# Moving output stores, gating steps and adapter preparation in a fused attention and mixture-of-adapters kernel

## The chip, the cores and the metric

The kernel runs on one core of a Trainium2 chip. The time is device microseconds of one launch. A core has five engines that each work through an instruction list of their own, in order: TensorE (PE, its weight loads shown apart as PEld), VectorE (DVE), ScalarE (ACT), GpSimd (POOL) and SyncE (SP, which here only issues DMAs). They wait for each other through semaphores. DMAs can be issued from the queues of SP, ACT and POOL.

## The reference

Two stages. The first is attention with a relative position bias, for 8 batches, 8 heads, 576 positions and 64 values per head. The second sends each of the 4608 rows of 512 values through the two best of 8 low-rank adapters (rank 16) and adds the result to the row.

```python
scores = scale * np.matmul(q, k.transpose(0, 1, 3, 2))
scores = scores + bias.transpose(2, 0, 1)[None]     # bias_table[bucket(|i - j|)], per head
attn = softmax(scores)                              # over the last axis
x = np.matmul(attn, v).transpose(0, 2, 1, 3).reshape(B * S, H * D)
logits = x @ w_gate                                 # 8 adapters
topk = two largest logits of each row; w = softmax of these two
out = x + sum over the two: w * ((x @ A[e]) @ B[e])
```

## The kernel before, in words

**Units and slots.** The work is cut into 32 units, one for each batch and pair of heads (four units to a batch). A unit has six slots, s0 to s5. The program is written out slot by slot, by hand, in a loop over `t` (192 slots); every engine gets its instructions in that order. `scores` opens each slot: matmuls into one of two PSUM buffers `sc`, and one exponential on ACT that empties it. Slots s0, s1, s3 and s4 have the large exponential (128x1024, line 344), s2 the `pe` tile of the last 64 keys (line 363), s5 the remaining 64 queries (line 348). In unit 0 the small ones come in the other order.

**What follows the scores.** The bias is a multiplication of the exponentials by a table `eb` (line 374, DVE, both operands bfloat16 in SBUF, 512 or 768 elements per partition; `bias_tail` at 383). The table is made once: a row `gx` goes to DRAM (`gx_d`, line 731, ACT's queue) and comes back spread over the partitions (`table_load`, line 193, SP). `values` (line 409) multiplies probabilities and values in half-tiles of 64 keys; `whole` (line 431) does so with 128 keys at once and was used for the last unit alone. `normalise` (441, 442) divides by the row sums.

**Loads.** SP issues all loads of q, k and v, 128 KB for a head as a rule, in the order in which `load` lists them, two or three to a slot. Staging has two buffers a batch long. POOL casts to bfloat16 into `qkn` (line 146), `vm` (151), `qke` (156) and `ve` (159), in program order; from unit 4 on, `cast_v(u)` stands in s1, the q part of unit u + 2 in s2 and its k part in s3. PE transposes them (283) in the slots before their unit and DVE copies the result out (287).

**Adapters.** `load_adapters` fetches A (`Af`), the gate (`Gf`) and B (`Bf`), on SP, while the second batch is being loaded. `cast_adapters(0)` makes `A4` on POOL (lines 254, 256) in unit 4, s4. `order_pe` (264) puts A's rows into the order needed, with matmuls against a spread identity, and `order_out` (268, DVE) copies that to `AW`. Those four steps enter `queue` at unit 5, s0.

**The groups of the second stage.** When a batch is done its 4 or 5 row tiles form a `Group`. Its steps go into `queue`: `front` (transposes, 473 and 479), two `sums` (486, 495, then `MAX8` at 497 and the mask at 500), `turn` (transpose of the gated sums, 528 and 533) and `back` (537, then 558 on DVE into `ot`). PE takes one step in s0, s2 and s5; DVE does its part at the next of s0, s1, s3. `enqueue` puts `pauses`, or left-over steps of the group before, between them so that the gating can be done. The gating list is popped once a slot: `distances` on POOL (509 to 511) in the slot after the mask, `gates` two slots later, which holds the tanh on ACT (517) and three POOL operations (518 to 521).

**Stores.** `dl_out` puts a store into `stores`, and the end of the next slot issues it (line 553): on POOL's queue, in the last unit on SP's. `ot` has six buffers. After the last slot, `dl_own` and `Last` finish the last rows.

Of the kernel before, what the change touches and what calls it, by code (L numbers as in the profile page):

```python
# [14 lines left out]
ALU = mybir.AluOpType  # L15
# [18 lines left out]
def kernel(  # L34
# [56 lines left out]
    def load(b):  # L91

        q32 = stg.tile([128, 4, H, D], FP32, name="q32", tag="q32")
        k32 = stg.tile([128, 4, H, D], FP32, name="k32", tag="k32")
        v32 = stg.tile([128, 4, H, D], FP32, name="v32", tag="v32")
        qke32 = stg.tile([128, H, D], FP32, name="qke32", tag="qke32")
        ve32 = stg.tile([128, HP, D], FP32, name="ve32", tag="ve32")
        staged[b] = (q32, k32, v32, qke32, ve32)
        sync = nc.sync.dma_start

        def tiles(t, src, h, j0=0, j1=4):
            return lambda: sync(out=t[:, j0:j1, h, :], in_=src[  # L102
                b, h, j0 * 128:j1 * 128, :].rearrange("(j p) d -> p j d", p=128))
# [12 lines left out]
        tail_qk = [lambda i=i, src=src: sync(out=qke32[i * 64:(i + 1) * 64],  # L116
                                             in_=src[b, :, 512:, :].rearrange("h p d -> p h d"))
                   for i, src in enumerate((q, k))]
        tail_v = [lambda i=i: sync(out=ve32[i * 64:(i + 1) * 64], in_=v[
            b, :, 512:, :].rearrange("(g two) p d -> two p g d", two=2)[i]) for i in range(2)]  # L120
        table = lambda hp: [lambda: table_load(hp)]
        values_left[b] = (values_of(2), values_of(3))
        if b:
            v2, v3 = values_left[b - 1]
            todo = v2 + (table(3) if b == 1 else []) + qk(0) + tail_qk + v3 + qk(1)
            if b == 1:
                todo += [lambda: load_adapters(0), lambda: load_adapters(1)]
            todo += values_of(0) + tail_v + qk(2) + values_of(1)
            if b == 1:
                todo += [lambda: load_adapters(2)]  # L130
            return todo + qk(3)
        return [lambda: nc.scalar.dma_start(
                    out=k32[:, 0, :2, :], in_=k[b, :2, :128, :].rearrange("h p d -> p h d")),
                tiles(q32, q, 0), tiles(q32, q, 1),
                lambda: nc.scalar.dma_start(out=btT, in_=bias_table.rearrange("b h -> h b")),
                tiles(k32, k, 0, 1), tiles(k32, k, 1, 1),
                *tail_qk, *qk(1), *values_of(0), *tail_v, *qk(2), None,
                *table(0), *table(1), *values_of(1), near_load, *qk(3), *table(2)]

    nats, tails = {}, {}  # L140

# [272 lines left out]
    def whole(u, j):  # L414

        b, hp = units[u]
        pm, pe = probs[u]
        vm, ve = vals[b % 2]
        if j == 4:
            accs[u] = pvp.tile([128, 2, 512], FP32, name="pv", tag="pv")  # L420
        pv = accs[u]
        for t in range(5):
            tok = min(t * 128, S - 128)
            for h in range(2):
                if j < 4:
                    lhsT = pm[:, h, j * S + tok:j * S + tok + 128]
                    rhs = vm[:, j, 2 * hp + h, :W]
                else:
                    keys = slice(h * 64, (h + 1) * 64)
                    lhsT, rhs = pe[keys, tok:tok + 128], ve[keys, hp, :W]  # L430
                nc.tensor.matmul(pv[:, h, t * W:(t + 1) * W], lhsT=lhsT, rhs=rhs,
                                 start=(j == 4 and t == 0), stop=(j == 3),
                                 skip_group_check=True)

    def normalise(u):
# [18 lines left out]


    queue, stores = deque(), []
    state = {"now": [], "last": None, "gating": []}

    class Group:
        def __init__(self, tiles):  # L460
# [30 lines left out]
        def zl_out(self, t0, n):  # L491
# [6 lines left out]
            if t0 + n == self.n:  # L498
                self.mk = self.tile("mk", E)
                nc.vector.tensor_tensor(self.mk, self.z[:, :, ER:], self.largest(1), op=ALU.is_ge)  # L500
                state["gating"] = [None, self.distances, None, self.gates]

        def largest(self, i):
            return self.top[:, :, i].to_broadcast((128, self.n, E))
# [1 line left out]
        def distances(self):  # L506
# [3 lines left out]
            eng.tensor_tensor(d2, lg, self.largest(1), op=ALU.subtract)  # L510
            eng.tensor_tensor(self.df, d1, d2, op=ALU.add)

        def gates(self):

            n, eng = self.n, nc.gpsimd
            th, d, gate = (self.tile(x, E) for x in ("th", "dm", "gate"))
            nc.scalar.activation(th, self.df, ACT.Tanh, scale=0.5)
            eng.tensor_tensor(d, th, self.mk, op=ALU.mult)
            eng.tensor_tensor(gate, d, self.mk, op=ALU.add)
            self.zt = self.tile("zt", ER, BF16).rearrange("p n (e r) -> p n e r", e=E)  # L520
            eng.tensor_tensor(
# [57 lines left out]
    def enqueue(tiles):  # L579
# [4 lines left out]
        steps = gr.front()  # L584
        sums1, sums2, turn = gr.middle()
        pauses = lambda n: [old.pop(0) if old else (None, None) for _ in range(n)]
        wait = 3 - len(steps) if tiles[0][0] else 3
        steps += pauses(wait) + [sums1, sums2] + pauses(7 - len(steps) - wait) + [turn]
        queue.extend(steps + old + gr.back())

    def step_pe():
        if queue:
# [127 lines left out]
            ready.append(units[p][0])  # L720

    loading = deque(todo + load(1))
    for t in range(SLOTS * NU):
        u, s = divmod(t, SLOTS)
        b, hp = units[u]
        p = u - 1
        early = u < HP
        done, stores[:] = stores[:], []
        scores(u, s)
        if t == 0:  # L730
            nc.scalar.dma_start(out=g, in_=gxe)
        if u == 0:
# [14 lines left out]
        if s == 0:  # L747
            if u == 1:
                cast_tail_v(0, pool_cast)
            if u == 5:  # L750
                queue.extend((lambda i=i: order_pe(i), lambda i=i: order_out(i))
                             for i in range(4))
            if u == 7:
                cast_adapters(1)
            if u in (1, 2):
                for j in range(2 * u - 2, 4):
                    bias(p, j)
                bias_tail(p)
            elif u:
                bias(p, 2)  # L760
# [27 lines left out]
        if s == 4:  # L788
            if u > 2:
                values(p, 1, 0, 1, 2, 3)  # L790
            if u == 4:
                cast_adapters(0)
            if early:
                transpose_pe(u + 1)
            elif u + 1 < NU:
                transpose_out(u + 1)
        if s == 5:
            if u in (1, 2):
                values(p, 1, 0, 1, 2, 3)
            if early:  # L800
                transpose_out(u + 1)
# [76 lines left out]
```

## Time and profile before

| | |
|---|---|
| median of 3 runs | 221.46 us (220.71 to 222.06) |
| the profiled execution | 221.52 us, of which the span 219.7 us |
| first exponential starts, last one ends | 7.5 us, about 201.2 us |
| busy: PE, DVE, ACT, POOL | 183.0, 172.6, 172.2, 107.1 us |
| large exponential (L344), each | 1.02 us, next one about 0.9 us after its start |
| POOL's stores (L553) | 27 issues, 559 ns each |
| granted TensorE clock, mean | 0.973 |
| DMA | 40.36 MB, 184 GB/s over the span |

A page row has the engine, what the group writes and reads, its count, its busy time and its idle time with what ended that. Three more views are used. The timeline lists instructions with their start and length and, in brackets, the idle time before them with its releaser. The view of waits sums who waited for whom. The windows view gives busy time, clock and DMA share of chosen stretches. A "unit" in the text starts at its first exponential on ACT.

### The profile page before, as it was taken

Reading aid. Unit: us, or ns where it says so; the run is one execution under the profiler, and the core shown is the slowest. Engines: PE = TensorE matmul, PEld = TensorE weight load, DVE = VectorE, ACT = ScalarE, POOL = GpSimd, SP = SyncE. Lnnn points to the kernel's source line nnn. Section 1 sums busy time; section 2 is a strip of 40 time slices with the busy share of each in tenths; the row PEclk is TensorE's granted clock in tenths of the full one; section 3 lists DMA queues with packets and bytes.
Section 4 is the critical chain, followed back from the end, with each engine's and each line's share of the span. In section 5 each row is a group of like instructions: output and inputs, shape, how many; then the busy total and the mean of one; then the engine's idle time right before and its main releaser. Section 6 shows DMA issues by size and latency. Waiting matters only on the chain.

```text
span 219.7 us, 10377 instructions
## 1 busy us (share of the span) xinstructions
PE 183.0 (83%) x4532; PEld 126.5 (58%) x4532; DVE 172.6 (79%) x356; ACT 172.2 (78%) x218; POOL 107.1 (49%) x203
## 2 busy tenths in 40 slices
PE   0869887299879999889995998989999998887851
PEld 0326565177657776557664765656777765666630
DVE  4327857138778989999989899999999999995460
ACT  4875889069779899879995899879998998888422
POOL 1562233634555729553968069535965495332010
PEclk9999999669999999999999999999999999999978
DMA  6999887989789979899898989998899421113406
GB/s 123 212 212 200 197 176 158 236 171 195 178 189 201 232 179 240 198 266 222 224 243 239 198 185 237 193 252 215 200 231 247 103 101 48 67 48 98 179 35 219
DMA packets 121189, 40.36 MB, mean 184 GB/s; under 512 B 116208, under 2 KB 118000, under 8 KB 121144
## 3 DMA queue, kind: packets, MB, share of 16 engines
q1 hardware_dynamic: 118560, 33.06, 67.6%
q0 software_dynamic: 2032, 6.56, 8.5%
q8 instruction: 35, 0.57, 1.1%
q10 hardware_dynamic: 552, 0.08, 0.2%
q14 instruction: 10, 0.08, 0.1%
HBM read 29.97 MB, written 9.45 MB: 179 GB/s over the span
## 4 chain that ended last, share of the span: by engine, by line
PE 44%; DVE 30%; SPq 15%; issue 4%; POOL 2%; ACT 2%; DMA 1%; DVEq 0%; ACTq 0%; POOLq 0%
DVE pm L374 14%; PE pv L409 11%; PE sc L334 10%; SPq L102 10%; DVE xn L442 4%; PE tp L283 4%; DVE ot L558 4%; PE xT_ps L473 3%; PE zl L486 3%; PE sc L356 3%; PE sc L317 2%; PE dl L537 2%; DVE qkT L287 2%; SPq L116 2%; DVE xT L479 1%
## 5 line engine op out<-in xcount | busy, mean ns | idle before, releaser
L344 ACT ACTIVATE pm<-sc 128x1024 bf16<-128x1024 f32 x128 | 127.4, 1023 | 29.3 <-PE sc L334 16.9
L374 DVE TENSOR_TENSOR pm<-pm,eb 128x768 bf16<-128x768 bf16 (+1 forms) x98 | 71.6, 754 | 6.7 <-DMA eb<-gx_d 3.3
L334 PE MATMUL sc<-qkT 64*128 64x64 bf16 (+1 forms) x512 | 62.6, 297 | 3.8 <-ACT pm L344 1.0
L409 PE MATMUL pv<-vm,pm 64*128 64x65 bf16 x2480 | 49.5, 191 | 1.4 <-DVE pm L374 1.3
L409 PEld LDWEIGHTS <-pm 64*128 64x128 bf16 x2480 | 44.6, 95 | 2.6 <-DVE pm L374 2.0
L334 PEld LDWEIGHTS <-qkT 64*128 64x128 bf16 x512 | 21.5, 94 | 25.6 <-issue 12.9
L146 POOL CAST qkn<-q 128x512 bf16<-128x512 f32 x31 | 21.2, 683 | 14.1 <-PE pv L409 4.7
L442 DVE TENSOR_TENSOR xn<-pv,rc 128x640 bf16<-128x640 f32 x32 | 26.4, 824 | 1.1
L553 POOL DMA_DIRECT2D out_dram<-ot x27 | 15.1, 559 | 24.6 <-DVE ot L558 24.6
L287 DVE COPY qkT<-tp 128x1024 bf16<-128x1024 bf16 x31 | 21.1, 680 | 6.6 <-PE tp L283 6.6
L317 PE MATMUL sc<-tb,turn 64*64 64x127 bf16 (+1 forms) x360 | 26.1, 218 | 0.0
L151 POOL CAST vm<-v 128x512 bf16<-128x512 f32 x32 | 21.4, 667 | 7.4 <-DMA v<-in_v_dram 7.4
L146 POOL CAST qkn<-k 128x512 bf16<-128x512 f32 (+1 forms) x32 | 20.0, 625 | 9.7 <-DMA k<-in_k_dram 9.7
L363 ACT ACTIVATE pe<-sc 128x576 bf16<-128x576 f32 x32 | 20.9, 654 | 2.5 <-PE sc L317 1.5
L283 PE MATMUL tp<-ident,qkn 128*128 128x128 bf16 x248 | 20.1, 226 | 0.0
L348 ACT ACTIVATE pm<-sc 128x512 bf16<-128x512 f32 x32 | 19.0, 593 | 0.3 <-PE sc L334 0.3
L283 PEld LDWEIGHTS <-qkn 128*128 128x128 bf16 x248 | 14.6, 100 | 7.5 <-issue 7.3
L317 PEld LDWEIGHTS <-turn 64*64 64x64 bf16 (+1 forms) x360 | 16.6, 99 | 3.6
L356 PE MATMUL sc<-qkT 64*64 64x64 bf16 (+1 forms) x128 | 16.3, 308 | 1.3 <-ACT pm L344 1.3
L509 POOL TENSOR_TENSOR da<-z,top 128x32 f32<-128x32 f32 (+1 forms) x7 | 1.8, 256 | 30.3 <-DVE top L497 30.3
L558 DVE TENSOR_TENSOR ot<-dl,xn 128x512 f32<-128x512 f32 x24 | 15.8, 681 | 0.0
L537 PE MATMUL dl<-Bc,zT 128*128 128x512 bf16 x31 | 12.0, 387 | 2.3 <-DVE zT L533 1.3
(110 smaller groups left out, 194.9 us busy)
## 6 DMA issues: line engine op xcount, KB each, us to landing
q<-in_q_dram SPq DMA_DIRECT2D x64, 128.0 KB, 4.1
k<-in_k_dram SPq DMA_DIRECT2D x62, 128.0 KB, 4.0
out_dram<-ot POOLq DMA_DIRECT2D x23, 256.0 KB, 4.1
v<-in_v_dram SPq DMA_DIRECT2D x32, 128.0 KB, 3.8
v<-in_v_dram SPq DMA_DIRECT2D x16, 256.0 KB, 5.4
out_dram<-ot SPq DMA_DIRECT2D x5, 256.0 KB, 2.2
qke<-in_q_dram SPq DMA_DIRECT2D x8, 128.0 KB, 5.0
qke<-in_k_dram SPq DMA_DIRECT2D x8, 128.0 KB, 4.4
```

The costliest lines, as they stand in the source:

```text
L102: return lambda: sync(out=t[:, j0:j1, h, :], in_=src[b, h, j0 * 128:j1 * 128, :].rearrange("(j p) d -> p j d", p=128))
L146: eng(out=nats[u][:, i, j0:j1].rearrange("p j (h d) -> p j h d", h=2), in_=staged[b][i][:, j0:j1, 2 * hp:2 * hp + 2, :])
L283: nc.tensor.transpose(ps[:, i, j, :], nats[u][:, i, j, :], ident)
L287: nc.vector.tensor_copy(batch_tiles(b)[:, hp, :, :512], tps.pop(u).rearrange("p i j t -> p i (j t)"))
L317: nc.tensor.matmul(out(a, e), lhsT=turn[rows, cols], rhs=tb[rows, hp, a - k0 + 127:e - k0 + 127], start=False, stop=True, skip_group_check ...
L334: nc.tensor.matmul(sc[:, h, o:o + n], lhsT=kT[rows, j * 128:(j + 1) * 128], rhs=qT[rows, q0:q0 + n], start=True, stop=True, skip_group_che ...
L344: nc.scalar.activation(pm[:, :, s * S:s * S + SW], sc, ACT.Exp, scale=scale)
L356: nc.tensor.matmul(flat[rows, q0:q0 + n], lhsT=kT[rows, 512:], rhs=qT[rows, q0:q0 + n], start=True, stop=True, skip_group_check=True)
L374: nc.vector.tensor_tensor(t, t, e, op=ALU.mult)
L409: nc.tensor.matmul(pv[:, h, t * W:(t + 1) * W], lhsT=lhsT, rhs=rhs, start=(j == js[0] and t == 0 and not cross), stop=(j == 3 and cross == 1),
L442: nc.vector.tensor_tensor(_ap(xs[b], hp * 128, [[D, 2], [Dm, 5], [1, D]]), _ap(pv, 0, [[512, 2], [W, 5], [1, D]]), _ap(rc, 0, [[5, 2], [1, ...
L558: nc.vector.tensor_tensor(ot, self.dl.pop(t), self.x[t], op=ALU.add)
```

## The change

1. Stores are issued from ACT's queue, two slots after they are made and behind that slot's exponential; the last unit's stores too. Only the stores behind the last slot stay on SP. POOL issues none.
2. Gating: `distances` stands one slot later, and the tanh is a step of its own, two slots behind it (one slot later than before; in the last unit as before). The POOL part of `gates` follows one slot behind the tanh.
3. Adapters: the loads of A and gate stand behind unit 6's q and k (before: ahead of that batch's first v), and B's behind unit 7's. `cast_adapters(0)` moves from unit 4, s4 to unit 5, s4, so behind the casts `vm`(5), q(7) and k(7) on POOL; B's cast moves from unit 7 to 8. The four order steps are no longer queued at unit 5: they stand in the first group's own list, between its transposes and its sums. This puts the first at unit 6, s0, and the group's first `sums` and its `turn` later too.
4. Unit 0's values: one run of `whole` in unit 1, s5 (50 matmuls) in place of `values` in s2 and s5 (100). The tile j = 0 comes first.
5. At the start, the first table load stands ahead of the two k loads of unit 2 (before: behind them).

```diff
@@ load @@
             todo = v2 + (table(3) if b == 1 else []) + qk(0) + tail_qk + v3 + qk(1)
+            todo += values_of(0) + tail_v + qk(2)
             if b == 1:
                 todo += [lambda: load_adapters(0), lambda: load_adapters(1)]
-            todo += values_of(0) + tail_v + qk(2) + values_of(1)
+            todo += values_of(1) + qk(3)
             if b == 1:
                 todo += [lambda: load_adapters(2)]
-            return todo + qk(3)
+            return todo
...
-                *tail_qk, *qk(1), *values_of(0), *tail_v, *qk(2), None,
-                *table(0), *table(1), *values_of(1), near_load, *qk(3), *table(2)]
+                *tail_qk, *qk(1), *values_of(0), *tail_v, *qk(2)[:2], None,
+                *table(0), *qk(2)[2:], *table(1), *values_of(1), near_load, *qk(3), *table(2)]
@@ Group @@
-                state["gating"] = [None, self.distances, None, self.gates]
+                state["gating"] = [None] * state["apart"] + [self.distances, None, self.tanh, self.gates]
...
+        def tanh(self):
+            self.th = self.tile("th", E)
+            nc.scalar.activation(self.th, self.df, ACT.Tanh, scale=0.5)
+
         def gates(self):
...
-            nc.scalar.activation(th, self.df, ACT.Tanh, scale=0.5)
-            eng.tensor_tensor(d, th, self.mk, op=ALU.mult)
+            eng.tensor_tensor(d, self.th, self.mk, op=ALU.mult)
@@ enqueue @@
-        wait = 3 - len(steps) if tiles[0][0] else 3
-        steps += pauses(wait) + [sums1, sums2] + pauses(7 - len(steps) - wait) + [turn]
-        queue.extend(steps + old + gr.back())
+        if tiles[0][0]:
+            steps += pauses(3 - len(steps)) + [sums1, sums2] + pauses(4)
+        else:
+            steps += [(lambda i=i: order_pe(i), lambda i=i: order_out(i)) for i in range(4)]
+            steps += [sums1, sums2] + pauses(3)
+        queue.extend(steps + [turn] + old + gr.back())
@@ the loop over slots @@
+    waiting = deque([[], []])
...
-        done, stores[:] = stores[:], []
         scores(u, s)
+        for st in waiting.popleft():
+            st(nc.scalar)
...
-            if u == 5:
-                queue.extend((lambda i=i: order_pe(i), lambda i=i: order_out(i))
-                             for i in range(4))
-            if u == 7:
+            if u == 8:
                 cast_adapters(1)
+            if u == NU - 1:
+                state["apart"] = 1
...
-            if u in (1, 2):
+            if u == 2:
                 values(p, 0, 0, 1, 2, 3, 4)
...
-            if u == 4:
+            if u == 5:
                 cast_adapters(0)
...
-            if u in (1, 2):
+            for j in range(5 if u == 1 else 0):
+                whole(p, j, 0)
+            if u == 2:
                 values(p, 1, 0, 1, 2, 3)
...
-        for st in done:
-            st(nc.gpsimd if u < NU - 1 else nc.sync)
+        waiting.append(stores[:])
+        del stores[:]
...
-    while stores:
-        stores.pop(0)(nc.sync)
+    for st in [x for w in waiting for x in w] + stores:
+        st(nc.sync)
```

More of the change, by code (lines that the diff above doesn't have):

```diff
@@ L412, in values, with whole @@
                                      skip_group_check=True)
-    def whole(u, j):
+    def whole(u, j, first=4):
         b, hp = units[u]
@@ L418, in whole @@
         vm, ve = vals[b % 2]
-        if j == 4:
+        if j == first:
             accs[u] = pvp.tile([128, 2, 512], FP32, name="pv", tag="pv")
@@ L431, in whole @@
                 nc.tensor.matmul(pv[:, h, t * W:(t + 1) * W], lhsT=lhsT, rhs=rhs,
-                                 start=(j == 4 and t == 0), stop=(j == 3),
+                                 start=(j == first and t == 0), stop=(j == (3 if first else 4)),
                                  skip_group_check=True)
@@ L456 @@
     queue, stores = deque(), []
-    state = {"now": [], "last": None, "gating": []}
+    state = {"now": [], "last": None, "gating": [], "apart": 2}
     class Group:
@@ L511, in distances @@
             eng.tensor_tensor(self.df, d1, d2, op=ALU.add)
+        def tanh(self):
+            self.th = self.tile("th", E)
+            nc.scalar.activation(self.th, self.df, ACT.Tanh, scale=0.5)
         def gates(self):
             n, eng = self.n, nc.gpsimd
-            th, d, gate = (self.tile(x, E) for x in ("th", "dm", "gate"))
-            nc.scalar.activation(th, self.df, ACT.Tanh, scale=0.5)
-            eng.tensor_tensor(d, th, self.mk, op=ALU.mult)
+            d, gate = (self.tile(x, E) for x in ("dm", "gate"))
+            eng.tensor_tensor(d, self.th, self.mk, op=ALU.mult)
             eng.tensor_tensor(gate, d, self.mk, op=ALU.add)
```

## The prediction

> **What bounds the kernel now.** I read the windows view first: PE, DVE and ACT are each busy for 8 to 10 us of every 10, and no busy total is near 219.7 us, so the time lies in waits. The exponentials on ACT run through the whole span, and in the timeline of ACT a unit without a wait lasts 5.05 us (unit 15 starts at 103.24, unit 16 at 108.30, unit 17 at 113.35). 32 such units make 162 us; from the first exponential (7.49) to the end of the last (201.2) it is 194 us. Some 32 us are gaps on ACT, and I went through these by unit. The view of waits gives the largest:
>
> ```profile
> ACT pm L344 <- PE sc L334: 16.9, 25, 5.0
> PE Ap L264 <- POOL A L256: 4.9, 1, 4.9
> ```
>
> The longest ACT wait (5.0 us) is the same event as the one wait of PE for POOL's cast of A. The timeline shows what POOL did before it:
>
> ```profile
> 39.19 0.61 POOL L146 CAST qkn<-q 128x512 bf16<-128x512 f32 x1 [3.01 <-DMA q<-in_q_dram]
> 40.52 0.61 POOL L146 CAST qkn<-k 128x512 bf16<-128x512 f32 x1 [0.71 <-DMA k<-in_k_dram]
> 41.42 1.01 POOL L254 CAST A<-Af 128x128 bf16<-128x128 f32 x4
> 42.63 0.61 PE L264 MATMUL Ap<-A,spread 128*128 128x136 bf16 x4 [4.90 <-POOL A L256]
> 43.83 1.02 ACT L344 ACTIVATE pm<-sc 128x1024 bf16<-128x1024 f32 x1 [4.98 <-PE sc L334]
> ...
> 45.47 0.62 POOL L146 CAST qkn<-k 128x512 bf16<-128x512 f32 x1 [1.04 <-DMA k<-in_k_dram]
> ```
>
> A's cast stands behind the casts of unit 6's q and k, which wait for their loads; PE, in order, holds the scores of unit 5, s1 behind it. The first 50 us are paced by loads: windows of the DMA share give 0.92, 1.03, 0.83 for the first three stretches of 10 us and 1.01 for 38 to 44.
>
> The second kind of gap comes later, at unit starts: 0.75 at 90.85, 1.38 at 97.62, 2.67 at 121.36, 0.75, 1.37, 0.75, 0.94 at 138.33, 145.09, 183.36, 189.68; together 8.6 us. The longest, with what DVE and POOL did ahead of it:
>
> ```profile
> 115.51 4.12 DVE L374 TENSOR_TENSOR pm<-pm,eb 128x512 bf16<-128x512 bf16 x2
> 115.84 0.62 POOL L146 CAST qkn<-q 128x512 bf16<-128x512 f32 x1
> 116.39 0.54 POOL L553 DMA_DIRECT2D out_dram<-ot  x1
> 116.93 0.62 POOL L146 CAST qkn<-k 128x512 bf16<-128x512 f32 x1
> 117.48 0.62 POOL L151 CAST vm<-v 128x512 bf16<-128x512 f32 x1
> 118.04 0.62 POOL L146 CAST qkn<-q 128x512 bf16<-128x512 f32 x1
> 118.60 0.61 POOL L146 CAST qkn<-k 128x512 bf16<-128x512 f32 x1
> 121.36 1.02 ACT L344 ACTIVATE pm<-sc 128x1024 bf16<-128x1024 f32 x1 [2.67 <-issue]
> ```
>
> Two bias multiplications, 0.41 and 0.55 us when POOL is still, take 4.12 us while POOL works off a backlog; DVE then copies the next unit's q and k late, and ACT waits. Beside casts alone the same pair loses far less:
>
> ```profile
> 81.53 1.33 DVE L374 TENSOR_TENSOR pm<-pm,eb 128x512 bf16<-128x512 bf16 x2
> 81.64 0.81 POOL L146 CAST qkn<-q 128x512 bf16<-128x512 f32 x1
> 82.40 0.94 POOL L156 CAST qke<-qke 128x512 bf16<-128x512 f32 x1
> ```
>
> I sorted the 79 bias multiplications after 50 us by what POOL ran beside them, and summed what each took beyond 0.55 us. 28 with POOL idle: 0.0 us. 24 beside compute alone: 4.0 us, 0.17 each. 27 beside a store issue (L553): 17.7 us, 0.66 each, up to 2.2. Every loss of more than one POOL operation has a store issue at its head.
>
> **The change part by part.**
>
> *Early table, unit 0's values in one run.* In the timeline SP issues the table load at 11.44 and DVE gets it at 15.82; ahead of the two k loads (0.51 us each) it comes 1.0 to 1.2 us earlier. PE no longer stands before unit 1, s3 for it (ACT gap 3.15 us at 18.84), and 50 matmuls of some 20 ns fall away. Unit 2 could start 2.2 us earlier. But the loads set a floor: unit 4's k is cast at 28.70 and unit 5's at 33.63, both with a DMA wait, and a cast (0.62), transposes (0.62), copy (0.68) and scores (0.4) put the first exponential 2.5 us behind. Unit 5 then starts at about 36.5 against 37.82. Whatever is won is lost in the next wait, so I count nothing for this part. If that wait is gone, unit 7's k sets the time (first rival).
>
> *The adapters.* The wait of 4.9 us goes from unit 5, s0, but the order of POOL's list puts A's casts behind q(7) and k(7), and PE needs them at unit 6, s0. When? k(7) is cast at 45.47, just after it lands; 256 KB of B no longer precede it, 1.1 us at the 237 GB/s of that window, so it lands at 44.3. Its cast and the five of A (41.42 to 42.58) end at 46.1. The first order matmuls then run at 46.1, where they ran at 42.63: 3.5 us later, but one unit (5.05 us) further in the program. That wins 1.6 us. PE comes out of this wait slow as before (the granted clock is 0.71 and 0.72 in 38 to 44 and 44 to 50); in s2 there stand 4 order matmuls (0.61 slow) in place of 8 transposes (1.04 slow), 0.4 us more. The sums of the first group used to wait for `AW` (0.7 us of PE); they now have a step of distance, and I take 0.5. The tanh of the first group still stands only two slots of PE ahead of `turn`, so ACT's gap of 1.28 us at 65.68 moves to unit 9 and remains. Sum: 2.5 us won, between 1 (the load is no earlier) and 8 (no wait).
>
> *Stores off POOL.* POOL loses 27 x 0.559 = 15.1 us, and 24.6 us of standing at its head for DVE's `ot`, which is what heaped the casts up. At 0.17 instead of 0.66 us, the 27 multiplications give DVE 13 us. Of this only the gaps count: 8.6 less the usual 0.22 at each of 7 starts is 7.1 us. Units 15 and 16 bear 0.4 to 0.5 us of losses within 5.05 us, so most of what stays is covered; I take 6.2, with 1.5 and 7.1 as ends.
>
> *Stores on ACT.* 30 issues. No store is issued by ACT before, so bounds: the nearest row is this one, an issue on ACT's queue inside an exponential, the next of which starts on time.
>
> ```profile
> 7.49 1.02 ACT L344 ACTIVATE pm<-sc 128x1024 bf16<-128x1024 f32 x1 [0.24 <-PE sc L334]
> 7.58 0.29 ACTq L731 DMA_DIRECT2D gx_d<-gxe  x1
> 8.41 1.02 ACT L344 ACTIVATE pm<-sc 128x1024 bf16<-128x1024 f32 x1
> ```
>
> SP's store at 205.32 took 0.36 us, and its loads between 0.5 and, with the DMAs full, 2.00 us (87.28). At 0.36 an issue is covered by the exponential ahead of it (0.5 us at least from start to next start). Three pairs of half stores, 0.5 to 0.6 each on SP, stand behind a short exponential or ahead of the last unit's tanh; I take 0.9 us lost in all, between 0 and 30 x 1.5 = 45. The wait they add holds the next exponential behind it; in the trace each `ot` ends at least 0.25 us before the exponential ahead of its store would start (two slots on), so it costs nothing unless DVE falls back by a slot.
>
> *Gating.* POOL casts q (and `qke`) before it stands for the maxima (30.3 us in 7 waits) and then stands for the tanh, a slot later. POOL's three products end about where they did (zt at 86.65, PE there at 86.5), so nothing. Two steps of the first group's `back` move from units 8 and 9 to 11 and 12: 2 x 0.68 us on DVE in units with less room, 0.4 lost.
>
> **The sum.** 2.5 + 6.2 - 0.9 - 0.4 = 7.4 us. The profiled execution took 221.52 us (span 219.7 and 1.8 around it), the median of the runs is 221.46. **221.5 - 7.4 = 214.1 us**.
>
> **The rivals.**
>
> *No wait for A* (12%). If A's casts are done when PE comes to unit 6, units run behind k(7): 44.3 + 2.5 puts unit 7 at 47.5 in place of 53.2, 5.6 us more: 208.5. Against it stands POOL's order; for it, that loads might land sooner.
>
> *Casts, not stores, hold DVE up* (20%). POOL is then released sooner, but its burst of six casts is as long and merely moves. Only 1.5 of the 6.2 us come: 218.8. For it: four casts in a row passed the multiplication at 116.9. Against it: the 24 cases without a store. The Trainium skill ("SBUF — State Buffer", Who interferes with whom) speaks for this rival: a VectorE operation with two SBUF inputs and a GpSimd one that reads SBUF block each other for a whole instruction, while issuing DMAs needs only the write side, which such an operation does not take. By that rule the sum is the 218.8 of this rival. The trace agrees as far as single losses go (above, the second multiplication waits for the end of the first cast, 82.45, and ends at 82.86); the losses of two to four operations behind a store it does not explain.
>
> *ACT pays for the stores* (8%), the slower end. If an issue on ACT is held up by full DMAs as SP's are, it outlasts the exponential. The gain without this term is 8.3 us, 0.28 for each of 30 stores, so it decides from about 0.8 us an issue (0.5 covered). At 1.0 us: 15 us, 221.5 - 8.3 + 15 = 228. Against: SP's long issues come when several loads of its own are under way, and ACT's queue would be nearly empty.
>
> **How the numbers follow.** Forecast 55%, by itself 212 to 216.5; the three rivals 12, 20 and 8; 5% for a result near the old time. The range 208.5 to 219.5 leaves out the last rival and some of the first. A measurement of this kernel tells 0.5% (1.1 us) from no change: faster 0.85 (forecast, first rival, most of the second), within 0.06, slower 0.09.
>
> **What would show it.** In the new trace: PE's wait for A at unit 6, s0, ending near 46 us, and unit 7 at about 53; no bias multiplication above 1.1 us after 50 us except beside `zt`, and unit starts 13, 14, 18, 21, 22 with gaps near 0.3; ACT's issues at 0.3 to 0.4 us inside exponentials. I am wrong if A is ready at 42 us, if multiplications still take 2 us beside plain casts, or if ACT has gaps behind its stores.

## The result and the profile after

The changed kernel is slower: 234.66 us median of 4 runs (234.07 to 235.04), against 221.09 us for the kernel before on the same chip. The ratio is 1.061, with an interval of 1.056 to 1.066. The profiled execution has a span of 232.5 us (before 219.7) and a mean granted clock of 0.913 (0.973). A few executions of a kernel are some per cent longer whatever it does; times, differences and ratios below are of the others alone, of which e11 has too few for a ratio and the kernel before, in the round of e1 to e4, only three of thirteen (median 218.3 us; of all thirteen 221.5).

The view of waits of the changed kernel has entries for ACT that the kernel before does not have (engine and line, what it waited for, us in total, times, longest):

```profile
ACT pm L345 <- DMA v<-in_v_dram: 6.0, 2, 3.6
ACT pm L345 <- DMA q<-in_q_dram: 3.5, 1, 3.5
ACT pm L345 <- DVE mk L501: 3.2, 1, 3.2
```

An exponential reads PSUM and has no business with a load of v or q. The timeline of the changed kernel shows what stands between them (start, length, engine, line):

```profile
98.36 1.02 ACT L345 ACTIVATE pm<-sc 128x1024 bf16<-128x1024 f32 x1 [0.21 <-PE sc L335]
98.86 2.02 SPq L102 DMA_DIRECT2D q<-in_q_dram  x2
102.16 0.34 ACTq L557 DMA_DIRECT2D out_dram<-ot  x1
102.23 0.19 DVE L501 TENSOR_TENSOR mk<-z,top 128x32 f32<-128x32 f32 x1
102.54 1.02 ACT L345 ACTIVATE pm<-sc 128x1024 bf16<-128x1024 f32 x1 [3.16 <-DVE mk L501]
...
159.67 1.02 ACT L345 ACTIVATE pm<-sc 128x1024 bf16<-128x1024 f32 x1
163.85 0.40 ACTq L557 DMA_DIRECT2D out_dram<-ot  x1
164.29 1.02 ACT L345 ACTIVATE pm<-sc 128x1024 bf16<-128x1024 f32 x1 [3.60 <-DMA v<-in_v_dram]
```

ACT stands still for 3.2 and 3.6 us, then issues one store in 0.34 or 0.40 us, and only then goes on. The store is short, as predicted; it is what it waits for that is long. The load of q that SP issued at 98.86 landed at 102.08, and the store started at 102.16. The releaser named in the first bracket (DVE's mask) cannot be it, as the mask starts behind the store; the store's own `ot` had ended at 97.29.

The program's instruction lists tell why that load matters. These are three issues with the semaphores that they wait for:

```
before, POOL  L553 DMACopy out_dram<-ot 128x512          [waits DMASW4_49,DVE_49]
after,  ACT   L557 DMACopy out_dram<-ot 128x512          [waits DMAHW2_49,DVE_49]
after,  SP    L102 DMACopy q32_338<-in_q_dram 128x4x64     [waits DMAHW2_49]
```

The DMAs of SP and of ACT share eight completion semaphores, DMAHW0 to 7, which the program hands out in turn; I call them lanes. Each DMA waits until the one that had its lane before, eight places earlier in the built program's order of these DMAs, has landed. POOL's stores had lanes of their own (DMASW), so before the change no store on POOL waited for a load. Now a store on ACT waits for a load, and in-order ACT holds the exponentials behind it. In the profiled execution six gaps on ACT of over 0.3 us (15.3 us together) stand ahead of a store, and the stores in them start 0.02 to 0.08 us after the landing of the DMA eight places earlier. After the last load (landed at 169.9) there is none: units 25 to 30 take 5.1 to 5.7 us.

The gaps are 15.3 us of what the change costs; the rest, as I read it, follows from ACT's standing still. The windows view of 100 to 120 us gives busy time and count of PE, PEld, DVE, ACT and POOL, then the granted clock, the DMA share and GB/s; first the changed kernel, then e1 (below), which differs only in the stores' queue:

```profile
100.00:120.00 20.00, 13.10 (x287) 9.38 (x282) 9.57 (x20) 11.49 (x14) 9.21 (x18) 0.75 0.98 220
```

```profile
100.00:120.00 20.00, 19.77 (x533) 13.98 (x526) 18.68 (x37) 18.78 (x24) 14.79 (x27) 1.00 1.00 241
```

The DMA engines are full in both, but ACT gets through 14 instructions in place of 24, and PE, busy for 13.1 of the 20 us, works at a granted clock of 0.75. In the chain of work that ended last, SP's queue has the largest share after the change:

```profile
SPq 32%; PE 29%; DMA 17%; DVE 5%; POOL 5%; issue 5%; ACT 4%; ACTq 1%; POOLq 0%
```

The pair of bias multiplications that took 4.12 us in unit 17 of before does what the prediction wanted, though; it has no POOL work beside it now:

```profile
123.11 0.88 DVE L375 TENSOR_TENSOR pm<-pm,eb 128x512 bf16<-128x512 bf16 x2
```

### The profile page after: what moved, and what is told of

The parts are those of the page before. It is cut to its first block, busy times and chain, and to the rows that moved or that the text cites. A ratio compares the mean times of both kernels' runs of the same rounds, so it can differ in the third digit from the quotient of the medians.

```text
span 232.5 us, 10288 instructions
## 1 busy us (share of the span) xinstructions
PE 185.8 (80%) x4478; PEld 132.9 (57%) x4492; DVE 160.3 (69%) x356; ACT 172.6 (74%) x218; POOL 91.6 (39%) x176
## 4 chain that ended last, share of the span: by engine, by line
SPq 32%; PE 29%; DMA 17%; DVE 5%; POOL 5%; issue 5%; ACT 4%; ACTq 1%; POOLq 0%
SPq L102 18%; PE sc L335 7%; DMA k<-in_k_dram 7%; PE pv L410 6%; SPq L113 5%; DMA v<-in_v_dram 4%; SPq L116 4%; ACT pm L345 3%; PE tp L284 3%; DMA q<-in_q_dram 3%; SPq L119 3%; PE sc L357 2%; DMA out_dram<-ot 2%; PE sc L318 2%; PE xT_ps L474 2%
## 5 line engine op out<-in xcount | busy, mean ns | idle before, releaser
L335 PE MATMUL sc<-qkT 64*128 64x64 bf16 (+1 forms) x512 | 65.7, 310 | 15.3 <-ACT pm L345 9.9
L375 DVE TENSOR_TENSOR pm<-pm,eb 128x768 bf16<-128x768 bf16 (+1 forms) x98 | 57.2, 599 | 19.4 <-ACT pm L345 17.2
L147 POOL CAST qkn<-q 128x512 bf16<-128x512 f32 x31 | 20.0, 646 | 26.0 <-issue 13.2
L147 POOL CAST qkn<-k 128x512 bf16<-128x512 f32 (+1 forms) x32 | 22.5, 702 | 13.2 <-DMA k<-in_k_dram 13.2
L318 PE MATMUL sc<-tb,turn 64*64 64x127 bf16 (+1 forms) x360 | 27.4, 224 | 0.0
L152 POOL CAST vm<-v 128x512 bf16<-128x512 f32 x32 | 20.4, 638 | 13.7 <-DMA v<-in_v_dram 13.7
L284 PE MATMUL tp<-ident,qkn 128*128 128x128 bf16 x248 | 21.6, 237 | 0.0
L284 PEld LDWEIGHTS <-qkn 128*128 128x128 bf16 x248 | 15.8, 106 | 7.7 <-issue 6.9
L442 DVE RECIPROCAL rc<-pv 128x10 f32<-128x10 f32 x32 | 7.0, 219 | 14.7 <-PE pv L410 12.9
L357 PEld LDWEIGHTS <-qkT 64*64 64x64 bf16 x128 | 8.1, 112 | 14.9 <-issue 9.6
```

The costliest lines, as they stand in the source:

```text
L147: eng(out=nats[u][:, i, j0:j1].rearrange("p j (h d) -> p j h d", h=2), in_=staged[b][i][:, j0:j1, 2 * hp:2 * hp + 2, :])
L284: nc.tensor.transpose(ps[:, i, j, :], nats[u][:, i, j, :], ident)
L318: nc.tensor.matmul(out(a, e), lhsT=turn[rows, cols], rhs=tb[rows, hp, a - k0 + 127:e - k0 + 127], start=False, stop=True, skip_group_check ...
L335: nc.tensor.matmul(sc[:, h, o:o + n], lhsT=kT[rows, j * 128:(j + 1) * 128], rhs=qT[rows, q0:q0 + n], start=True, stop=True, skip_group_che ...
L357: nc.tensor.matmul(flat[rows, q0:q0 + n], lhsT=kT[rows, 512:], rhs=qT[rows, q0:q0 + n], start=True, stop=True, skip_group_check=True)
L375: nc.vector.tensor_tensor(t, t, e, op=ALU.mult)
```

## The experiments: is it the stores on ACT?

**e1: the changed kernel with the stores back on POOL.**

```diff
         for st in waiting.popleft():
-            st(nc.scalar)
+            st(nc.gpsimd)
```

> The changed kernel with one line undone: its stores are issued from POOL's queue again, still two slots after `ot`. Theory (lanes): on ACT a store must wait until the DMA that stands eight places before it among SP's and ACT's DMAs in the program has landed, and that is mostly a load that SP issues late; the exponentials stand behind it. On POOL the stores use other semaphores, so ACT's stalls ahead of stores (15.3 us in seven of them in the profiled run of the changed kernel) go, and with them the cold PE behind them: 215 to 219 us. DVE's bias multiplications beside a store's issue lose time again (22.5 us of excess over 0.55 us before, 7.8 us after: here near 20). Rival (the other parts of the change cost the time: the gating behind more slots, the adapters ordered in the first group, the first values in one run): it stays at 228 us or more.

213.7 us (213.1 to 215.0), ratio to before 0.977 (0.964 to 0.991), and 21.0 us under the changed kernel: less than I expected. ACT has no gap ahead of a store. The other expectation failed too: what the bias multiplications take beyond 0.55 us comes to 11.8 us and not to near 20 (before 22.5, changed kernel 7.8), although POOL issues the stores again.

**e2: the kernel before with its stores on ACT**, two slots after `ot`, those of the last unit too; nothing else.

```diff
-        done, stores[:] = stores[:], []
         scores(u, s)
+        for st in waiting.popleft():
+            st(nc.scalar)
...
-        for st in done:
-            st(nc.gpsimd if u < NU - 1 else nc.sync)
+        waiting.append(stores[:])
+        del stores[:]
```

> The kernel before with one part of the change alone: stores issued from ACT's queue, two slots after `ot`, the last unit's from SP. Theory (lanes): the stores alone make the kernel slow: 230 to 238 us, with single gaps of 1 to 4 us on ACT ahead of stores while loads still run, each ended within 0.1 us of the landing of the DMA eight places earlier. Rival (the stores are a gain, as predicted, and another part costs the time): 213 to 219 us.

237.3 us, ratio 1.085 (1.070 to 1.100): 19.0 us more than before. Ten gaps, 19.9 us. With e1 this settles which part makes the kernel slow.

**e4: the stores on SP's queue**, among the loads (`st(nc.sync)`).

> The changed kernel with the stores issued from SP's queue, among the loads, two slots after `ot` as the program has it. Theory (lanes): a store waits for the same landing eight places earlier as on ACT, but SP has no exponential behind it, only loads for units far ahead; ACT has no stall ahead of a store, POOL's port is free of stores: 212 to 217 us. Rival (a store that waits holds up the loads behind it on SP, and these come too late for the casts): ACT's waits move to casts and transposes, 222 us or more.

218.4 us, ratio 1.000 (0.993 to 1.007). ACT is free of stores, but neither bound was met, and the rival has a point: stores now queue behind SP's loads, `ot` comes free late, and DVE stands for it. The timeline of e4:

```profile
100.74 0.69 DVE L562 TENSOR_TENSOR ot<-dl,xn 128x512 f32<-128x512 f32 x1 [5.98 <-DMA out_dram<-ot]
101.49 1.01 PE L284 MATMUL tp<-ident,qkn 128*128 128x128 bf16 x8 [5.56 <-DVE ot L562]
```

That one wait costs ACT 6.5 us in unit 14. So it was not the casts that came late, as the rival had it, but the six `ot` buffers that ran out.

## The experiments: can the loads be placed so that the wait goes?

If a store waits because SP is behind its place in the program, loads written later or more evenly should free it. Five kernels tried this with the stores on ACT, three of them with a control on POOL.

**e3**: eight loads a unit from unit 8 on in place of twelve. **e5**: also begun one unit later.

```diff
-        for i in range(3 if u < 2 else 2):
+        for i in range(3 if u < 2 else 2 if u < 8 or s % 3 == 0 else 1):   # e3; u < 7 in e5
...
-        if hp == 1 and s == 5 and b + 2 < B:
+        if hp == (2 if b else 1) and s == 5 and b + 2 < B:                 # e5
```

> The changed kernel, with SP's loads written into the program more evenly: from unit 8 on eight loads a unit in place of twelve, so that a unit's batch no longer stands in the program long before the DMA engines get to it. Stores stay on ACT. Theory (lanes): the DMA eight places ahead of a store has then mostly landed when ACT comes to it: the gaps ahead of stores fall from 15.3 us to under 4 and the time to 212 to 219 us. Rival (an issue on ACT costs by itself, whatever landed before it): the gaps stay, 230 us or more.

> The changed kernel, stores on ACT, with the loads' places in the program moved back: from unit 7 on eight loads a unit as in e3, and the loads of a batch begin one unit later than in e3 (batches 3 to 7). In e3 SP stayed behind the program although the loads were spread, since the DMA engines were 0.87 to 1.06 busy from 80 to 160 us and a backlog that is once there isn't worked off. Theory (lanes): with the loads one unit later in the program SP comes to a store's place in the program no later than ACT, the DMA eight places earlier has landed, and the gaps ahead of stores of over 0.3 us, 15 us in the changed kernel, fall under 6 us: 214 to 222 us. Rival (the DMA engines are full, and a store on ACT waits for them wherever the loads stand in the program): the gaps stay over 12 us, 230 us or more.

234.1 us (ratio 1.070, 1.039 to 1.100) and 231.7 us (1.043, 1.032 to 1.054), with gaps ahead of stores of 19.8 and 17.9 us. Both miss what I expected.

**e9**: loads of batches 3 to 7 begun three units later. **e10**: the same, stores on POOL.

```diff
-        if hp == 1 and s == 5 and b + 2 < B:
-            loading.extend(load(b + 2))
+        if u == 1 and s == 5:
+            loading.extend(load(2))
+        if hp == 0 and s == 5 and 2 <= b < B - 1:
+            loading.extend(load(b + 1))
```

> The changed kernel, stores on ACT, with the loads of batches 3 to 7 begun three units later in the program (at two a slot as in the changed kernel). The last load is issued at 166 to 177 us in every run so far; the exponentials are then in unit 23.8 where ACT stores (the changed kernel, e2, e3), in 24.5 in e5, and in 26.7 to 28.5 where POOL does. Theory (lockstep: with stores in its queue ACT cannot get past the place that the loads have in the program, and the loads go at the DMA engines' pace): the place of the last load moves from unit 24 to 27, the exponentials may be three units further when it is issued (near 26.5 to 28), and the time falls by about 3 units of 5.5 us: 215 to 221 us, gaps ahead of stores under 7 us. Rival (a store on ACT waits wherever the loads stand): as e3 and e5, 230 us or more.

> e9 with the stores on POOL: what the later loads do by themselves. Lockstep theory: the loads come at the DMA engines' pace and just in time already, so their place in the program costs nothing without stores on ACT: 212.5 to 216 us, as e1. Rival (the later place starves the DMA engines or the casts): 218 us or more, and then e9 can't get under that.

228.7 us (1.031, 1.020 to 1.041) and 216.8 us (0.981, 0.972 to 0.990), e10 just above its expected range. The exponentials are in unit 26.8 when the last load is issued, as expected, but at 180.6 us, and the gaps are 13.7 us. Half a success; the expected time was missed.

**e13**: e9 with seven loads a unit from unit 9 on. **e14**: the same on POOL. **e17** and **e18**: these two with the copy `xe<-xn` on POOL's queue.

```diff
+        for i in range(3 if u < 2 else 2 if u < 9 or s == 0 else 1):       # e13, e14, e17, e18
...
-            nc.sync.dma_start(out=xe[b // 2][:64, :], in_=xs[b][64:, 4, :])
+            nc.gpsimd.dma_start(out=xe[b // 2][:64, :], in_=xs[b][64:, 4, :])   # e17, e18
```

> e9 (stores on ACT, loads of batches 3 to 7 begun three units later in the program), and from unit 9 on seven loads a unit in place of twelve. In e9 the gaps ahead of stores stood in units 14, 15 and 23, where a burst of 24 to 28 loads is written into 12 to 14 slots (12 us) that the DMA engines need 17 us for; in units 18 to 22, outside the bursts, there were none over 0.25 us. Lockstep theory: without bursts the DMA eight places ahead of a store stands nearly seven slots back and has landed: gaps ahead of stores from unit 10 on under 5 us together (13.7 in e9), 215 to 222 us, within 4 us of e14. Rival (a store on ACT waits for full DMA engines wherever the loads stand): gaps over 10 us, 228 us or more.

> e13 with the stores on POOL, its control: 213 to 218 us if the place of the loads costs little, as in e10 (217.1). Rival (loads that are written so late come too late for the casts): over 220 us, and e13 with it.

e13: 231.4 us (1.044, 1.036 to 1.052); e14: 219.0 (0.989, 0.982 to 0.995), just above its expected range. e13 was no clean test. Its timeline shows SP standing at the copy of `xn` for 7 us, with the loads of the next batch behind it:

```profile
83.19 1.18 SPq L102 DMA_DIRECT2D k<-in_k_dram  x2
91.63 0.51 SPq L449 DMA_DIRECT2D xe<-xn  x1
```

> e13 with the copy xe<-xn issued from POOL's queue, so that SP's loads wait for nothing but landings and buffers. Lockstep theory: SP is no longer behind its place in units 10 to 27, the gaps ahead of stores of over 0.3 us come to under 5 us (11.6 in e13) and the time to within 5 us of e18: 214 to 222 us. Rival (a store on ACT waits for full DMA engines wherever the loads stand): gaps of 10 us or more, 228 us or more.

> e17 with the stores on POOL, its control. Theory: the DMA engines no longer stand idle from 84 to 92 us, so 1 to 5 us sooner than e14 (219.0): 213 to 218 us. Rival (POOL stands at the copy until xn is there and its casts come late): 219 us or more.

e17: 237.0 us (1.068, 1.057 to 1.079), about as slow as e2; e18: 214.0 (0.965, 0.956 to 0.974). The last load, which the kernel writes in unit 28, is issued while ACT is in unit 23.8, so that SP seems to be ahead, and the theory of the place seems to fall. But e17 does not test it. The built program hands out the lanes in an order of its own, which is not always the written one (what sets it, I do not know). In e17 ten of the eleven stores that end a gap have the lane of a load that the kernel writes behind them, by 3 to 22 slots; in the six other kernels with stores on ACT it is four of 53. One such load, written 6 slots behind its store, is in e17's timeline:

```profile
80.21 1.06 SPq L102 DMA_DIRECT2D k<-in_k_dram  x2
82.28 0.59 ACT L349 ACTIVATE pm<-sc 128x512 bf16<-128x512 f32 x1
86.36 0.37 ACTq L557 DMA_DIRECT2D out_dram<-ot  x1
86.83 1.94 ACT L345 ACTIVATE pm<-sc 128x1024 bf16<-128x1024 f32 x2 [3.97 <-DMA k<-in_k_dram]
```

The second of the two loads of k, issued at 80.76, had the store's lane. It landed at 86.29, with the DMA engines at a share of 1.03 between 80 and 100 us, and the store went 0.07 us later. What the pairs have in common:

| stores on ACT / control on POOL | times, us | difference | gaps over 0.3 us ahead of stores | unit of ACT at the last load's issue |
|---|---|---|---|---|
| changed kernel / e1 | 234.7 / 213.7 | 21.0 | 15.3 us | 23.8 / 28.3 |
| e2 / before | 237.3 / 218.3 | 19.0 | 19.9 us | 23.8 / 26.7 |
| e9 / e10 | 228.7 / 216.8 | 11.9 | 13.7 us | 26.8 / 28.2 |
| e13 / e14 | 231.4 / 219.0 | 12.4 | 11.6 us | 26.8 / 28.2 |
| e17 / e18 | 237.0 / 214.0 | 23.0 | 21.9 us | 23.8 / 27.0 |

In the seven profiled kernels with stores on ACT, 64 stores end such a gap. 60 of them start 0.02 to 0.08 us after the landing of the DMA eight places earlier, and in 63 that DMA is one of SP's, 2.5 to 6.6 us after its issue. So the wait for the lane is shown, in all seven kernels. The last column fits it: in the order of the lanes, the first store on ACT behind the last load is written in unit 23, s5 in the changed kernel, e2 and e17 and in unit 27, s3 in e9 and e13, and ACT had not passed that place when the last load was issued. That some arrangement of the loads frees ACT is not shown: e13 came to 11.6 us of gaps at the least, and e17 did not move the loads behind the stores. Stores on ACT with lanes apart from the loads' were not tried.

## The experiments: what do the other parts do?

e1 is quicker than before although its stores are on POOL, where I had put the loss. Four kernels made from the one before, with one part each:

**e6: the gating alone**, stores from POOL as before (first group: products where they were, differences a slot sooner; `apart` is 0 up to unit 10, then 2, in the last unit 1).

```diff
-                state["gating"] = [None, self.distances, None, self.gates]
+                state["gating"] = [None] * state["apart"] + [self.distances, None, self.tanh, self.gates]
```

> The kernel before with the gating's part of the change alone: the differences two slots later from the second group on, the tanh in a slot of its own ahead of the products (in the first group the differences a slot sooner, the products where they were); stores from POOL a slot after `ot`, as before. e1 is 5.3 us better than before behind unit 10, where only the gating and the stores' second slot can act. Theory (gating): these are the gating's, since POOL's differences no longer stand in front of casts and waiting for DVE's maxima: 215 to 218 us. Rival (the stores' second slot, as POOL no longer waits for `ot`): 220.5 to 222.5 us, as my prediction priced the gating.

211.9 us, ratio **0.955** (0.949 to 0.960), 10.0 us under before: the quickest kernel of the study, ahead of before and after, and better than expected.

**e7: the stores' second slot alone**, on POOL.

> The kernel before with its stores two slots after `ot` in place of one, still from POOL's queue, and nothing else (the last unit's go from SP). Theory (gating): next to nothing, 219.5 to 222 us. Rival (the second slot): POOL reaches a store when `ot` has long ended, its casts are not held up, and DVE meets fewer stores: 215 to 218 us.

222.2 us, ratio 1.001 (0.998 to 1.005). It says less than I meant it to: POOL issues nothing between the end of one slot and the start of the next, so up to the last unit its list is the same as before. The rival was not tried by it.

**e11 and e12: the gating's two halves**, from the second group on.

```diff
+                    state["gating"] = [None, None, self.distances, self.gates]               # e11
+                    state["gating"] = [None, self.distances, None, None, None, self.gates]   # e12
```

> The kernel before; from the second group on (not in the last unit) the gating's differences a slot later, behind two casts on POOL, the products where they were, still ahead of the stores. Theory (order of products and stores: in units 12, 20 and 28 of before a store issue stood right behind the zt product, where the bias multiplications of 2.45 us run; e6 moved that store ahead of the products): little of e6's gain, 218.5 to 222 us. Rival (POOL's wait for DVE's maxima in front of the casts was the loss): 212 to 216 us.

> The kernel before; from the second group on (not in the last unit) the tanh and the gating's products two slots later, behind a store on POOL, the differences where they were. Theory (order of products and stores): nearly all of e6's gain, 211.5 to 215 us. Rival (the wait for the maxima ahead of the casts): 218.5 to 222 us.

e11: four executions of 221.5 to 226.7 us, no ratio; no gain is to be seen. e12: 216.8, ratio 0.978 (0.971 to 0.986). The products' place behind the stores gives half of e6's gain by itself. The differences' place gives nothing alone; it may give the other half together with it, but e6 also has the tanh a slot ahead of the products and another order in the first group, which e12 leaves out, and these were not tried apart. The theory (nearly all from the products) was half right.

What the products' place does is seen in unit 20. The timeline of before:

```profile
132.60 1.53 POOL L521 TENSOR_TENSOR zt<-z,gate 128x640 bf16<-128x640 f32 x1
133.34 3.45 DVE L374 TENSOR_TENSOR pm<-pm,eb 128x512 bf16<-128x512 bf16 x2
134.08 0.57 POOL L553 DMA_DIRECT2D out_dram<-ot  x1
134.65 0.62 POOL L151 CAST vm<-v 128x512 bf16<-128x512 f32 x1
135.20 0.62 POOL L146 CAST qkn<-q 128x512 bf16<-128x512 f32 x1
```

and of e6:

```profile
125.58 0.54 POOL L556 DMA_DIRECT2D out_dram<-ot  x1 [0.25 <-DVE ot L561]
127.40 1.47 POOL L524 TENSOR_TENSOR zt<-z,gate 128x640 bf16<-128x640 f32 x1
128.09 1.95 DVE L374 TENSOR_TENSOR pm<-pm,eb 128x512 bf16<-128x512 bf16 x2
128.83 0.80 POOL L151 CAST vm<-v 128x512 bf16<-128x512 f32 x1
129.57 0.94 POOL L146 CAST qkn<-q 128x512 bf16<-128x512 f32 x1
```

In e6 the store is ahead of the products. The two multiplications take 1.95 us in place of 3.45, and now the casts wait for them (0.80 and 0.94 us where they had 0.62). The gaps at unit starts 13, 14, 18, 21, 22, 29 and 30, 8.6 us in before, are at most 0.22 each in e6, with all 27 stores on POOL.

**e8: e1 with two more pauses** ahead of the first group's `turn`, against the gaps of unit 9.

> e1 (the whole change, with stores on POOL) and two more pauses ahead of the first group's last turn of z. In e1 PE waits in unit 9 for POOL's products of the first group (gaps of 1.75, 1.03 and 0.85 us ahead of ACT's exponentials, zt done at 64.7). Theory: with the turn two steps later (at unit 9's third step or later) these gaps go, 2 to 3.5 us: 210 to 212 us. Rival (the gaps are the loads' and move to the next wait): 213 to 214 us.

214.0 us, ratio 0.964 (0.959 to 0.969): no better than e1, as the rival had it. Unit 10 starts at 69.8 in place of 71.9, and 0.6 us of these 2.0 are left at the last exponential.

**e15: the adapters alone** (with their loads and casts moved as in the change). **e16: the first values and the table alone.**

```diff
+        if tiles[0][0]:                                                    # e15
+            steps += pauses(3 - len(steps)) + [sums1, sums2] + pauses(4)
+        else:
+            steps += [(lambda i=i: order_pe(i), lambda i=i: order_out(i)) for i in range(4)]
+            steps += [sums1, sums2] + pauses(2)
...
+            for j in range(5 if u == 1 else 0):                            # e16
+                whole(p, j, 0)
```

> The kernel before with the adapters' part alone: their loads ahead of values and scores of later heads, the ordering of A as four steps of the first group, the casts a unit later. My prediction's 2.5 us: 218.5 to 219.5 us. Theory now (the loads' rate: the last load is issued at 171 to 175 us in every kernel with stores on POOL, and 19 to 22 us after it the exponentials end in all the quicker ones, so that what is won early is lost again at later loads): within 1.5 us of before, 220 to 222.5 us, though unit 8 starts 2 us or more sooner.

> The kernel before with unit 0's values in one run of whole products and the table's loads earlier, nothing else. Predicted: nothing, 220 to 222 us. Rival: unit 2's earlier start (20.8 in place of 21.4 us in e1) lasts, 1 us or more sooner at the end.

e15: 217.8 us, ratio 0.984 (0.977 to 0.991), so 3.6 us, near the prediction and not near the theory that I had by then. e16: 221.7, ratio 1.005 (1.001 to 1.010): no gain.

## Why the prediction was wrong

The forecast was 214.1 us with 0.85 for faster; it is 234.7, outside the range. **The step that failed is the last sentence of "Stores on ACT"**: "The wait they add holds the next exponential behind it; in the trace each `ot` ends at least 0.25 us before the exponential ahead of its store would start (two slots on), so it costs nothing unless DVE falls back by a slot." I looked at the wait for `ot` and took it for the only one. An issue has a second wait, for its lane, and I costed it at nothing by not seeing it. Stores on ACT cost 12 to 23 us in the five pairs above.

Point by point:

- **Early table, first values: 0.** Right. e16 gives no gain, and unit 5 starts there at 36.4 (forecast 36.5).
- **The adapters: 2.5 us.** Near in size, 3.6 in e15. The place is right, the times are not: in the changed kernel k(7) is cast at 42.46 (forecast: landed at 44.3), PE's wait for A is this, in unit 6,

```profile
44.55 0.40 PE L265 MATMUL Ap<-A,spread 128*128 128x136 bf16 x4 [1.17 <-POOL A L257]
```

  ending at 44.55 and not at 46.1, and unit 7 starts at 49.8 and not at 53.2. Against that the gaps of unit 9, where the first group's `turn` waits for POOL's products, were mis-sized: 4.8 us of ACT's time in the changed kernel and 3.6 in e1, not 1.28.
- **Stores off POOL: 6.2 us.** Wrong. I had sorted the bias multiplications by what stood beside them and took "beside a store" for the cause. The trace of before already spoke against it: 6 of those 27 multiplications have a store's issue beside them and nothing else of POOL's, and they take no longer than with POOL idle; all of the 17.7 us is lost by the 21 that have POOL's casts or products beside them too. The timeline of before, with a pair at its idle time:

```profile
147.12 0.88 DVE L374 TENSOR_TENSOR pm<-pm,eb 128x512 bf16<-128x512 bf16 x2
147.50 0.54 POOL L553 DMA_DIRECT2D out_dram<-ot  x1 [3.67 <-DVE ot L558]
```

  In e6 the stores are where they were, and the gaps that I gave to them are gone. e1 and the changed kernel, with stores on POOL and without, take 38.9 and 38.7 us for units 25 to 31 (the loads are over by then in the changed kernel, in e1 only in unit 29): with the gating moved, the stores' leaving gains 0.2 us there.
- **Stores on ACT: 30 issues at 0.36 us.** Right for the issues: 0.33 to 0.41 us for single ones. Their wait is the failed step.
- **Gating: nothing.** Wrong, by 10.0 us. I looked only at when zt ends, not at what the move does to the order of stores, products and casts on POOL.

Without the move to ACT the change takes 213.7 us, and the forecast was 214.1. That is no merit of the sum: 6.2 us that I gave to the stores belong to the gating.

The rivals: "ACT pays for the stores" had the right side and place, but a wrong mechanism, issues of 0.8 us and more. "Casts, not stores, hold DVE up" was nearer than the forecast in its first half: the store's issue is not what holds DVE up. It drew on the Trainium skill ("SBUF — State Buffer", Who interferes with whom), by which issuing DMAs does not block a multiplication of two SBUF inputs. The traces agree: beside a store's issue alone, 6 multiplications in before and 11 in e6 take 0.55 us at most, as with POOL idle; so does one in e1 (at 190.56) that starts 0.21 us behind a store. With compute beside the store as well, 21 lose 0.84 us each in before, and 17 lose 0.23 each in e6. What makes this difference is not settled. In unit 21 POOL's list is the same in both kernels and the first multiplication starts 0.22 us behind the store in both. In before the cast behind the store goes first, in its usual 0.62 us, and the multiplication ends 0.49 us after it; in e6 the multiplication is done first and the cast takes 0.88. The pair takes 1.43 and 1.65 us in before, 0.78 and 0.96 in e6. The rival "No wait for A" has a slip in its sum: 44.3 + 2.5 is 46.8 and not 47.5, so by its own numbers it stood for about 207.7 us.

Two things more stay open. The parts' gains do not add up: 10.0 (e6) and 3.6 (e15) alone, together 4.6 in e1 and 7.9 in e8, each against the kernel before of its own round, though unit 10 starts 1.4 us sooner in e1 than in e6. And e12 and e11 do not tell what gives the other half of e6's gain.

## What to carry to other kernels

Before a DMA is moved to another queue, list every semaphore that its issue waits for, not only the one of its data, and ask whose landings these are: where an engine shares its DMA semaphores with a queue that keeps the DMA engines full, a store is as late as somebody else's load, and so is all that stands behind it. Read that order in the built program: it need not be the order of the source, as e17 shows. If an engine must issue DMAs itself, let it be one that can afford to stand (here POOL, whose semaphores are its own). A loss that goes with a neighbour in the trace is not yet that neighbour's doing; moving only the neighbour's order, as e6 and e12 did, costs one run.

## What the runs showed of the hardware

- DMAs of two engines can hold each other up through completion semaphores alone: 60 of 64 delayed stores went 0.02 to 0.08 us after the landing of a DMA that has nothing to do with them. The Trainium skill ("DMA: Bandwidth & Descriptors", Issuing engines are not separate DMA queues) says that issuing from several engines only saves the time of issuing. Here it agrees in that the issues are short (0.33 to 0.41 us), but which engine issues the stores made 21.0 us of difference between e1 and the changed kernel, and there the measurement decides.
- The loads that these stores waited for took 2.5 to 6.6 us from issue to landing; the page of the changed kernel has medians of 3.5 to 5.1 us for all loads.
- An output store's issue on POOL does not by itself hold up a multiplication of two SBUF inputs on DVE: the 17 that stand beside such an issue alone in before and e6 take 0.41 or 0.55 us, as with POOL idle.
- The order of a few small POOL operations (three products and a store, three differences and a tanh on ACT) was worth 10.0 us, on a kernel in which POOL is busy for half of the time.
